# Zero matmuls in all early waits of TensorE, a replanned instruction order, and token-order stores for the last batch, in an attention + MoE kernel

## Chip, cores, metric

One core of a Trainium2 chip; each job ran on one chip, and the jobs on several. The metric is device microseconds of one execution. Each profile is one execution, and its times count from the start of the span, which is some 1.8 us shorter than the measured time. The record calls every execution but one fast; the one called slow is of the kernel before (408.87 us at a mean granted TensorE clock of 0.98, which is the share of full clock that the throttle gave, in the job of e5 to e8), and ratios use fast runs alone. But the fast state still holds executions with a mean clock of 0.97 to 0.99; where a few tenths of a per cent matter, I give the clock and compare executions of 0.996 and more.

## The reference, cut to what matters

```python
# q, k, v: (8 batches, 12 heads, 448 tokens, 64), fp32
scores = q @ k.transpose(0, 1, 3, 2) / sqrt(64)
attn = exp(scores - max); attn = attn / attn.sum(-1)
x = (attn @ v).transpose(0, 2, 1, 3).reshape(3584, 768)
h = x @ w_in                      # 768 x 2048
out = (h * sigmoid(h)) @ w_out    # 2048 x 768
```

## The kernel before

Attention is cut into **units**: four heads of one batch, all 448 tokens (two pieces of 224 in the first batch). A unit takes, in order: K and Q turned on VectorE (KT, QT); scores on TensorE into one of two score banks (s); an exponential on ScalarE, which frees the bank (E); row sums and values on TensorE (a, "a<-E,ones" and "a<-E,V"); on VectorE the sums turned, inverted and turned back (sT, inv, rdn) and two products a x rdn = xT, which also free the banks of a. Then come the MoE matmuls (h<-xT,w_in_t), tanh and gate, and the products p and o, for which VectorE also makes combinations of weights (D) and of gates (S, G, X) so that fewer matmuls are needed.

No order is written by hand. While the program is built, a planner in Python simulates the engines with fixed durations and priorities and writes down in which order each engine gets its instructions:

```python
def act(n): return n * 0.000833 + 0.093      # planned length of a ScalarE instruction
...
elif best is None or at + op.bias < best[0]: # the ready instruction with the lowest (ready time + bias) goes next
    best = (at + op.bias, op)
...
op = Op("DVE", 0.72, lambda: turn_k(b, hg), [ld_k[(b, hg)]], 20)             # bias 20: late
od.add(Op("DVE", ..., lambda n=n, c=c: add_e(n, c), deps, -1))               # T = E + E
Op("DVE", busy, lambda step=step: inverse(n, step), made[-1:] + before[step], -1)   # sT, inv, rdn
Op("DVE", ..., lambda: norm(n, part), [op] + rdn_op[n], -1, then=m_ring.give)       # xT
...
# TensorE has nothing to do, early on: zeros keep its clock up
if warm["on"] and od.free["PE"] <= od.now and wait > 0.1 and od.now > 1.0:
    n = max(1, int((wait - 0.06) / mm(128)))
    od.on_pe(Op("PE", n * mm(128), lambda n=n: run_zeros(n)), "full")
```

Results go out per 32 tokens, because tokens are kept in an interleaved order:

```python
for w in range(4):                           # one tile of 128 tokens x 384
    eng = nc.scalar if w % 2 and 4 * qd + 4 == NT * B else nc.sync
    eng.dma_start(out=dst[col // 32], in_=ost_t[(qd, i, j)][32 * w : 32 * (w + 1), :])
```

The softmax here doesn't subtract the row's maximum and nothing guards it: scores larger than these inputs give would overflow.

## Time and profile before

| | before |
|---|---|
| time, median of 3 (range) | 403.28 us (403.15 to 403.38) |
| span of the profiled execution | 401.82 us |
| first scores / V landed / first matmul that reads V | 7.44 / 15.29 / 15.38 |
| 55th MoE matmul starts | 37.63 |
| last matmul ends | 396.92 |
| last add ends / last store lands / end | 397.52 / 400.54 / 401.82 |

How to read it: TensorE is busy 98% of the span, so I cut the span at points that both kernels have in common. Up to the first matmul that reads V the loads decide; from there to the 55th MoE matmul the attention of the first units; from there to the last matmul the real work of both kernels is the same (340.75 us of streaming); then comes the tail. In the third stretch I count two things besides streaming: changes between packings of the array (from matmuls that use it whole to matmuls that use strips of 32 of its rows or columns, or back; some 0.09 us each), and waits (bursts whose start comes over 0.25 us later than the columns ahead of it explain, less one change). These are sums over the trace's matmuls, so they are larger than the waits view alone, which gives the idle time without the latencies at its ends. The lines are in the prediction below.

### The profile page before, as it was taken

Reading aid. Unit: us, or ns where it says so; the run is one execution under the profiler, and the core shown is the slowest. Engines: PE = TensorE matmul, PEld = TensorE weight load, DVE = VectorE, ACT = ScalarE, POOL = GpSimd, SP = SyncE. Lnnn points to the kernel's source line nnn. Section 1 sums busy time; section 2 is a strip of 40 time slices with the busy share of each in tenths; the row PEclk is TensorE's granted clock in tenths of the full one; section 3 lists DMA queues with packets and bytes.
Section 4 is the critical chain, followed back from the end, with each engine's and each line's share of the span. In section 5 each row is a group of like instructions: output and inputs, shape, how many; then the busy total and the mean of one; then the engine's idle time right before and its main releaser. Section 6 shows DMA issues by size and latency. Waiting matters only on the chain.

```text
span 401.8 us, 9398 instructions
## 1 busy us (share of the span) xinstructions
PE 392.6 (98%) x3758; PEld 201.9 (50%) x3758; DVE 301.1 (75%) x646; ACT 234.2 (58%) x360; POOL 88.7 (22%) x160
## 2 busy tenths in 40 slices
PE   8999999999999999999999999999999999999995
PEld 7676754444444444444445444444345555555562
DVE  2566677999997986998866985986985765775763
ACT  3887886686865769457367519738767124123410
POOL 6643466523006350300170104300000000000000
PEclk9999999999999999999999999999999999999999
DMA  7999999947017943641191537411001220122014
GB/s 115 194 199 206 164 166 206 156 71 117 2 46 120 186 57 50 112 80 47 41 150 37 105 75 93 69 41 41 2 0 42 60 59 2 40 67 53 2 39 118
DMA packets 38506, 34.42 MB, mean 86 GB/s; under 512 B 11712, under 2 KB 37696, under 8 KB 38464
## 3 DMA queue, kind: packets, MB, share of 16 engines
q0 software_dynamic: 27712, 22.82, 39.2%
q1 hardware_dynamic: 10368, 10.63, 10.5%
q8 instruction: 29, 0.48, 0.5%
q10 hardware_dynamic: 384, 0.39, 0.4%
q14 instruction: 13, 0.11, 0.1%
HBM read 45.61 MB, written 11.01 MB: 141 GB/s over the span
## 4 chain that ended last, share of the span: by engine, by line
PE 92%; DMA 2%; DVE 2%; POOL 1%; ACT 1%; issue 1%; DVEq 0%; POOLq 0%
PE h L454 37%; PE p L545 30%; PE a L383 11%; PE s L319 11%; PE o L559 3%; DMA V<-in_v_dram 2%; ACT E L356 1%; DVE T L367 1%; POOL rk L237 0%; POOL rq L243 0%; DVE G L535 0%; DVE xT L440 0%; POOL V L256 0%; DVE ost L598 0%; ACT th L465 0%
## 5 line engine op out<-in xcount | busy, mean ns | idle before, releaser
L356 ACT ACTIVATE E<-s 128x896 f16<-128x896 f32 (+1 forms) x172 | 149.2, 914 | 47.5 <-PE s L319 46.2
L454 PE MATMUL h<-xT,w_in_t 128*128 128x448 f16 (+1 forms) x864 | 156.5, 332 | 0.1
L454 PEld LDWEIGHTS <-w_in_t 128*128 128x128 f16 x864 | 79.9, 98 | 70.5 <-issue 16.4
L465 ACT ACTIVATE th<-h 128x448 f16<-128x448 f32 (+1 forms) x144 | 71.6, 505 | 68.3 <-PE h L454 62.5
L501 DVE SCALAR_TENSOR_TENSOR G<-th,h 128x448 f16<-128x448 f16 (+2 forms) x144 | 75.3, 532 | 37.4 <-ACT th L465 35.9
L256 POOL DMA_DIRECT2D V<-in_v_dram x88 | 48.7, 570 | 101.6 <-PE a L383 86.6
L319 PE MATMUL s<-QT,KT 32*128 32x448 f16 (+4 forms) x864 | 55.1, 340 | 1.2 <-ACT E L356 1.2
L545 PEld LDWEIGHTS <-G 128*128 128x128 f16 x384 | 36.4, 98 | 29.1 <-issue 5.5
L545 PEld LDWEIGHTS <-S 128*128 128x128 f16 x312 | 29.1, 98 | 23.8 <-issue 5.8
L383 PE MATMUL a<-E,V 128*32 128x448 f16 (+3 forms) x864 | 40.3, 334 | 0.7 <-DMA V<-in_v_dram 0.7
L545 PE MATMUL p<-D,G 128*128 128x384 f16 x208 | 38.0, 326 | 0.4 <-DVE xT L440 0.4
L545 PE MATMUL p<-w_out_t,S 128*128 128x384 f16 x208 | 37.0, 326 | 0.0
L440 DVE SCALAR_TENSOR_TENSOR xT<-a,rdn 128x448 f16<-128x448 f32 (+1 forms) x54 | 28.9, 561 | 9.0 <-PE a L383 8.1
L545 PE MATMUL p<-w_out_t,G 128*128 128x384 f16 x176 | 31.8, 326 | 0.0
L367 DVE TENSOR_TENSOR T<-T,E 128x1792 f16<-128x1792 f16 x20 | 21.8, 1088 | 12.8 <-ACT E L356 12.7
L319 PEld LDWEIGHTS <-KT 32*128 32x128 f16 (+2 forms) x864 | 16.6, 98 | 28.2 <-issue 27.2
L383 PEld LDWEIGHTS <-V 128*32 128x32 f16 (+2 forms) x864 | 18.3, 95 | 23.4 <-issue 14.6
L367 DVE TENSOR_TENSOR T<-E,E 128x1792 f16<-128x1792 f16 x20 | 21.7, 1084 | 6.1 <-ACT E L356 6.0
L535 DVE TENSOR_TENSOR S<-G 128x512 f16<-128x512 f16 x70 | 25.1, 415 | 0.7 <-PE p L545 0.7
L237 POOL DMA_DIRECT2D rk<-in_k_dram x24 | 13.7, 569 | 54.1 <-DVE KT L293 46.5
L293 DVE STREAM_TRANSPOSE KT<-rk 128x256 f32<-128x256 f32 (+3 forms) x48 | 16.5, 382 | 7.5 <-DMA rk<-in_k_dram 7.0
L423 DVE STREAM_TRANSPOSE sT<-a 128x448 f32<-128x448 f32 (+1 forms) x27 | 15.8, 586 | 4.8 <-PE a L383 4.4
(41 smaller groups left out, 251.9 us busy)
## 6 DMA issues: line engine op xcount, KB each, us to landing
out_dram<-ost SPq DMA_DIRECT2D x216, 48.0 KB, 1.6
rk<-in_k_dram POOLq DMA_DIRECT2D x24, 224.0 KB, 5.2
rq<-in_q_dram POOLq DMA_DIRECT2D x21, 224.0 KB, 5.8
w_out_t<-in_moe_w_out_dram POOLq DMA_DIRECT2D x8, 384.0 KB, 11.7
V<-in_v_dram POOLq DMA_DIRECT2D x43, 64.0 KB, 4.5
V<-in_v_dram POOLq DMA_DIRECT2D x40, 48.0 KB, 4.1
w_in_t<-in_moe_w_in_dram POOLq DMA_DIRECT2D x6, 256.0 KB, 7.6
w_in_t<-in_moe_w_in_dram POOLq DMA_DIRECT2D x3, 512.0 KB, 13.1
```

What stands on the lines that cost most here:

```text
L256: nc.gpsimd.dma_start(out=VT[b].rearrange("p h c i e -> p h c (i e)")[32 * x : 32 * (x + 1), hs, 0:count], in_=v[b, hs].rearrange("h (i g) ...
L293: nc.vector.transpose(out=turned.rearrange("p c x i -> p x c i")[:, x:y, 0:count], in_=t[:, first : first + count * (y - x)].rearrange("p ...
L319: nc.tensor.matmul(out=pS[p0 : p0 + 32 * (x1 - x0), h % 2, at : at + nq], lhsT=KT[(b, hg)][32 * h : 32 * (h + 1), c, x0:x1, :, e], rhs=QT[ ...
L356: nc.scalar.activation(out=E[(n, w)][0:kr, 2 * y : 2 * y + 2, 0:nk], in_=pS_t[(n, w, y)][0:kr, :, 0:nk], func=AF.Exp, scale=attn_scale,)
L367: nc.vector.tensor_tensor(out=T_t[n], in0=E[(n, 0)] if c == 1 else T_t[n], in1=E[(n, c)], op=ALU.add,)
L383: nc.tensor.matmul(out=a[32 * h : 32 * (h + 1), 0:nq], lhsT=w, rhs=e[k0:k1, h, at : at + nq], start=start, stop=stop,)
L440: nc.vector.scalar_tensor_tensor(out=xT[(b, cc)][:, 32 * g0 : 32 * g1], in0=acc[(n, part)][:, 0:nq], scalar=0.5, in1=rdn_t[n].rearrange("p ...
L454: nc.tensor.matmul(out=h[:, 0 : t1 - t0], lhsT=w_in_t[:, cc, 128 * f : 128 * (f + 1)], rhs=xT[(b, cc)][:, t0:t1], start=(cc == 0), stop=(c ...
L465: nc.scalar.activation(out=th, in_=h_t[(b, f, t0)][:, 0 : t1 - t0], func=AF.Tanh)
L501: nc.vector.scalar_tensor_tensor(out=dst[:, f, at + lo : at + hi], in0=th_t[(b, f, t0)][:, lo - t0 : hi - t0], scalar=1.0, in1=h_t[(b, f, ...
L535: nc.vector.tensor_tensor(out=dst[:, f0:f1], in0=x[:, f0:f1], in1=y[:, f0:f1], op=op)
L545: nc.tensor.matmul(out=pr_t[(qd, BANK[m])][:, 0:OH], lhsT=w[:, f, :], rhs=W_[m][:, f, :], start=(f == 0 and BANK[m] == m), stop=(f == HF - 1),
```

## The change

Its intent: no idle TensorE before the MoE runs (zeros in every gap, but only 47 ahead of the first scores), an order planned with durations nearer to the chip's and with V later, and fewer, larger stores at the end. The diff, cut to its core:

```diff
 def act(n):
-    return n * 0.000833 + 0.093
+    return n * 0.000833 + 0.065
-    PACE = 3.4
+    PACE = 3.6
 # load_q: the last batch in token order, one load for each head
+        if b == B - 1:
+            for h in range(HG): nc.gpsimd.dma_start(out=t[32*h : 32*(h+1)], in_=q[b, HG*hg+h].rearrange("(g i) d -> i g d", i=32))
 # store: contiguous tokens
+            if b == B - 1:
+                n = 2 if last and i == j else 4 - w
+                dst = out[b * S + col : b * S + col + 32 * n, cols]
+            (nc.scalar if last and w else nc.sync).dma_start(out=dst, in_=ost_t[(qd, i, j)][32 * w : 32 * (w + n), :])
 # planner: V's load 1.12 times as long in the first batch, Q's loads of the last batch four times as long;
 # the first K turned in two parts, the first burst of scores undivided
 # biases on VectorE:
-turns of K and Q 20   combine_w 30   combine_g 0   add_e -1   inverse -1   norm (xT) -1    gate -0.3
+turns of K and Q  8   combine_w 100  combine_g 8   add_e  0   inverse  4   norm (xT) -10   gate -2
 # biases on ScalarE:
-tanh -2    copies -2
+tanh -0.3  copies -0.3
-                od.now >= pace["next"] or moe_i is None or len(moe) < 30
+                od.now >= pace["next"] or moe_i is None or len(moe) < 14
-                pace["next"] = min(max(pace["next"], od.now - 4), od.now) + ...
+                pace["next"] = min(max(pace["next"], od.now - 8), od.now) + ...
+                    if av_seq[0][0][0] < 9 and (x := qk_at()) is not None and x <= od.now + 0:
+                        break                       # scores ahead of values, first units
+    FIRST_ZEROS = 47
+    od.on_pe(Op("PE", FIRST_ZEROS * 2 * mm(128), lambda: run_zeros(FIRST_ZEROS)), "full")
-        if ... wait > 0.1 ...:      n = max(1, int((wait - 0.06) / mm(128)))
+        if ... wait > 0.05 ...:     n = max(1, int((wait - -0.06) / each))    # each: twice as long before 8 us
```

(The two lines of biases sum up single numbers that stand at their instructions.)

## The prediction

> **What bounds the kernel now.** I read the page first (busy shares, chain by engine), then the timeline of the first 30 us, the chain of waits up to 40 us, the waits of TensorE alone from 37.7 us on, and the timeline and the stores of the last 6 us.
>
> ```profile
> PE 392.6 (98%) x3758; PEld 201.9 (50%) x3758; DVE 301.1 (75%) x646; ACT 234.2 (58%) x360; POOL 88.7 (22%) x160
> ...
> PE 92%; DMA 2%; DVE 2%; POOL 1%; ACT 1%; issue 1%; DVEq 0%; POOLq 0%
> ```
>
> TensorE is the bound, and it is nearly gapless. So the change can only win where TensorE does no useful work: before V lands, at a few waits, at changes between packings of the array, and behind the last matmul. No matmul with data in it is removed.
>
> ```profile
> 1.03 6.47 PE L1157 MATMUL z<-zeros 128*128 128x128 f16 x73 [1.03 <-DVE zeros L214]
> ...
> 5.09 0.70 DVE L293 STREAM_TRANSPOSE KT<-rk 128x384 f32<-128x384 f32 x2 [4.12 <-DMA rk<-in_k_dram]
> 5.72 0.37 DVE L304 STREAM_TRANSPOSE QT<-rq 128x224 f32<-128x224 f32 x1
> ...
> 7.44 0.60 PE L319 MATMUL s<-QT,KT 32*128 32x224 f16 x16
> ...
> 8.05 7.62 ACT L356 ACTIVATE E<-s 128x896 f16<-128x896 f32 x9 [6.03 <-PE s L319]
> ...
> 15.38 0.57 PE L383 MATMUL a<-E,V 128*32 128x224 f16 x16 [0.69 <-DMA V<-in_v_dram]
> ...
> 16.49 0.92 ACT L356 ACTIVATE E<-s 128x896 f16<-128x896 f32 x1 [0.82 <-PE s L319]
> ```
>
> Two things stand in it. The first scores could start at about 6.1, when K and Q have been turned (5.72 + 0.37), but wait until 7.44 behind 73 zero matmuls. And whatever is won there meets a wall: V is not there before 15.0.
>
> ```profile
> 5.77 9.24 DMA V<-in_v_dram
> ...
> 34.18 0.81 ACT E L356
> ...
> 35.03 0.38 PE a L383 x6
> ...
> 37.53 0.83 PE h L454 x7
> ```
>
> The chain up to 40 us runs through the landing of V, not through the zeros or the first exponentials. From V on it is TensorE, then a second knot at 33 to 37.5: two exponentials of the sixth unit, its row sums, the chain of VectorE to its xT, and the MoE matmuls that need it.
>
> ```profile
> PE s L319 <- ACT E L356: 0.8, 2, 0.5
> PE p L545 <- DVE xT L440: 0.4, 1, 0.4
> ```
>
> These are all waits of TensorE after 37.7 that the waits view gives; with the latency at their ends they cost about 0.9 (at 57.8), 0.65 (at 77.7) and 0.55 (at 123.0), 2.1 us in all.
>
> ```profile
> 395.68 3.65 SPq L593 DMA_DIRECT2D out_dram<-ost  x7
> ...
> 396.73 1.74 ACTq L593 DMA_DIRECT2D out_dram<-ost  x4
> ...
> 396.96 0.56 DVE L598 TENSOR_TENSOR ost<-p,s 128x384 f32<-128x384 f32 x1 [0.26 <-PE p L545]
> ...
> DMA to landing us min/median/max: 1.5/1.7/2.0
> ```
> The last result is in SBUF at 397.52, yet the sync queue issues stores until 399.33; the last starts at 398.9, lands some 1.6 later at 400.5, and 1.3 us of closing follow.
>
> **What the Trainium skill says.** "TensorE: Matmul & The Clock Gate", section "What's actually happening": the array starts at half clock and gets the full one after about one window of 3.4 us of activity, and the window runs free of the kernel's start. The trace agrees in kind: the 73 zeros take 6.41 us, not 73 x 0.056 = 4.1, so about 44 of them ran at 0.107 (44 x 0.107 + 29 x 0.056 = 6.3); here it took 4.7 us. "Back-to-back issue gap" on that page gives columns / 2.4 GHz + 2.5 ns for a warm matmul; the trace agrees (448 columns every 0.189 us). "DMA: Bandwidth & Descriptors", section "Issuing engines are not separate DMA queues": several issuing engines save only issue time; section "Why small descriptors are slow (HBM only)": 256-byte pieces pay a fixed overhead each. The first fits the end of this trace, where issue time is what is queued; no load here has 256-byte source rows, so the second is not shown yet.
>
> **Part by part, start.** 47 zeros in place of 73: 44 cold and 3 warm are 44 x 0.107 + 3 x 0.056 = 4.9 us from 1.03, so they end near 5.95, still before Q is turned; K turned in two parts lets Q through some 0.3 earlier. The first scores then start near 6.1, **1.3 us earlier**. The loads, though, are issued in the same order with the same waits, so V should land at 15.0 again, and the built order has exactly the same real matmuls ahead of the first one that reads V (nine score bursts and one row sum). All of the 1.3 us turns into waiting, whether filled with zeros (93 of the 96 now stand before that point or in front of it) or not. After V I walked the new order burst by burst with the lengths of the old timeline (two score halves 0.70, 16 value matmuls 0.44, 32 of them 0.88, a half score burst 0.50 to 0.53, an exponential every 0.814): the first MoE matmul comes near 22.05 in place of 22.70, since one alternation of scores and values is gone and scores run in pairs. But the new order does all eight first MoE tiles before the sixth unit's row sums, so the two exponentials there lie bare: scores to 32.9, exponentials to 34.75, sums at 34.8 against 35.03. From there on the work left is again identical in both kernels (340.75 us of streaming). So of 1.3 us about **0.25** arrives.
>
> **Middle.** From there to the last matmul the old kernel takes 359.3 us: 340.75 streaming, 2.1 of waits, and 16.4 that 186 changes of packing account for, 0.088 each (a check: 24 MoE matmuls of 224 columns should take 2.30 and the next scores start 2.40 after them). The built order now has 189 changes: **+0.27**. For waits I looked for scores that follow scores too closely. A burst needs both score banks back, which is two exponentials: about 2.4 us from start to start (75.99 to 78.38). The old order has pairs planned 1.70 and 1.72 apart, and those are its two score waits. The new one has the same two, and two more of 1.87 and 2.0. That makes about 2.25 us of waits: 0.7 + 0.65 + 0.5 + 0.4. The xT wait at 123 (0.55) should go, as xT now comes first on VectorE. Middle together about **+0.4**. Against that, the planner's figures are nearer to the chip: an exponential of 896 is planned at 0.811 (it was 0.839; measured 0.814), so orders chosen with it should hold fewer waits that I don't see. For this I take off **0.4**, as a judgement.
>
> **Last batch.** Q in token order takes four loads in place of one for three units, in 256-byte pieces: 9 more issues of about 0.57 on GpSimd. The old kernel loads the last Q at 254.8 and turns it at 282.8; 28 us of slack hide that. K and V need no order. The stores get contiguous tokens: the last four tiles go as 8 stores less. The last two tiles take one store of 96 KB on each of two queues, issued at once when the last add ends. That puts the last landing at about 2.2 us after the add (1.7 to 2.0 for 48 KB, plus some 0.3 for twice the bytes), where it was 3.0: **-0.8**.
>
> **Sum.** 403.28 - 0.25 + 0.4 - 0.4 - 0.8 = 402.2.
>
> **Rivals.** (1) The early start carries through: -1.3 in place of -0.25, total about 401.1. For it: in both kernels TensorE is full from V on. Against: same work before V, same V. It needs V to land earlier, and nothing issued before V changes. (2) The new order removes nearly all waits, as it was made with better figures: another -1.8, near 400.5. For it: two of the figures were clearly off (cold zeros, exponentials). Against: the same close pairs are in the new order, and tanh (0.455 to 0.50 for 448 columns, planned 0.438) and the copies (0.505, planned 0.385) are now planned further from the truth. (3) A wait replaces a wait: the bare exponentials before the sixth unit and the two new close pairs cost more than I give them, or lower priority for sums on VectorE starves products: +1 to +1.5, so 403.5. (4) The tail gains little since a store of 96 KB takes as long as two of 48: +0.5.
>
> **Range and chances.** The sizes are all below 2 us and partly cancel; I give each of start, middle and tail an error of 0.5 to 0.9, so 400.7 to 403.6. Two per cent is 8.1 us. Even without a wait after V: 15.4, then 355.7 of streaming, some 213 changes at 0.088, 2.3 for the half-packed score bursts of the first units, 4.1 from the last matmul to the end and 1.5 that the measured time has over the span (403.28 against 401.8) make 397.7. So faster by over 2% (under 395.2) is next to impossible, and nothing in sight costs 8 us either.
>
> **What would show it.** Right: first scores near 6.1, V again at 15.0 to 15.4, first MoE matmul near 22, the sixth unit's sums ending near 35.1, score waits near 46, 58 and 78, last landing 2.0 to 2.4 after the last add. Wrong: a V that lands at another time, the sixth unit's knot passed over 0.7 us earlier or later, TensorE waits after 37.7 of under 1 or over 3.5 us in sum, or a last store still queued behind others.

## The result, and the profile after

**404.77 us** median of 4 (404.38 to 405.50), where the kernel before took 403.21 (402.74 to 403.38) beside it: 1.0043 times as long, 95% interval 1.0024 to 1.0061. Ratios here are the mean time of one kernel's fast runs over that of the other's of the same rounds, so not quite the ratio of the medians quoted. By the measure of 2% that is "same"; against the prediction it is 2.6 us late and 1.2 us outside the range.

| us | before | after | difference | predicted |
|---|---|---|---|---|
| first scores | 7.44 | 5.72 | -1.72 | -1.3 |
| first matmul that reads V | 15.38 | 14.47 | -0.91 | 0 |
| from there to the 55th MoE matmul | 22.25 | 22.97 | **+0.72** | -0.25 |
| from there to the end of the last matmul | 359.30 | 361.06 | **+1.76** | 0.0 (+0.4 - 0.4) |
| last matmul to the end of the span | 4.90 | 4.17 | -0.73 | -0.8 |
| span | 401.82 | 402.67 | +0.85 | -1.05 |

The rows from "reads V" on sum to the last: -0.91 + 0.72 + 1.76 - 0.73 = +0.84. The -0.91 is not the change's doing: in the profiles of kernels that load in this order (15 of the 17 here), V's last part lands anywhere from 14.0 to 15.6.

Timeline of TensorE in the kernel after (start, length, engine, line, operation, tiles, shapes, count, and in brackets the idle time ahead and what ended it):

```profile
1.03 4.22 PE L1186 MATMUL z<-zeros 128*128 128x128 f16 x47 [1.03 <-DVE zeros L214]
5.72 0.58 PE L330 MATMUL s<-QT,KT 32*128 32x224 f16 x16 [0.47 <-DVE QT L315]
...
14.47 0.57 PE L394 MATMUL a<-E,V 128*32 128x224 f16 x16 [0.57 <-DMA V<-in_v_dram]
...
19.73 0.76 PE L394 MATMUL a<-E,V 128*32 128x224 f16 x22
21.14 0.47 PE L394 MATMUL a<-E,V 128*32 128x224 f16 x10 [0.65 <-issue]
21.54 0.60 PE L330 MATMUL s<-QT,KT 32*96 32x224 f16 x8
22.07 1.32 PE L465 MATMUL h<-xT,w_in_t 128*128 128x224 f16 x12
...
34.83 0.37 PE L394 MATMUL a<-E,ones 96*32 96x224 f16 x6 [0.53 <-ACT E L367]
```

The scores start when Q is there, and V is the wall again: TensorE stands 0.57 before it even with zeros. New is the line with `[0.65 <-issue]`: in the middle of a burst of 32 equal matmuls TensorE stands for 0.65 us, and nothing that the profile shows holds it. The kernel before runs the same kind of burst in one piece.

Waits of TensorE from 37.5 us on, kernel after (who waits, for whom, us in total, times, longest); the same view of before had two lines, 0.8 and 0.4:

```profile
PE h L465 <- DVE xT L451: 1.3, 3, 1.0
PE a L394 <- DVE xT L451: 0.5, 1, 0.5
PE p L556 <- DVE S L546: 0.3, 1, 0.3
PE h L465 <- DVE sT L434: 0.3, 1, 0.3
PE s L330 <- ACT E L367: 0.2, 1, 0.2
```

ScalarE was the first cause before; now all but 0.2 is VectorE. With the latencies at their ends the waits come to 3.58 us in place of 2.12, and there are 189 changes of packing in place of 186: 1.46 + 3 x 0.09 = 1.73 of the 1.76. The largest is at 76.7. VectorE there, kernel after:

```profile
74.99 0.64 DVE L304 STREAM_TRANSPOSE KT<-rk 128x256 f32<-128x256 f32 x2
76.37 0.62 DVE L451 SCALAR_TENSOR_TENSOR xT<-a,rdn 128x448 f16<-128x448 f32 x1 [0.74 <-PE a L394]
76.91 0.64 DVE L443 STREAM_TRANSPOSE rdn<-inv 128x448 f32<-128x448 f32 x1
77.47 0.60 DVE L315 STREAM_TRANSPOSE QT<-rq 128x448 f32<-128x448 f32 x1
78.00 1.12 DVE L451 SCALAR_TENSOR_TENSOR xT<-a,rdn 128x448 f16<-128x448 f32 x2
```

TensorE meanwhile, kernel after:

```profile
76.75 0.93 PE L465 MATMUL h<-xT,w_in_t 128*128 128x448 f16 x4
78.64 0.35 PE L465 MATMUL h<-xT,w_in_t 128*128 128x448 f16 x1 [0.96 <-DVE xT L451]
79.17 0.35 PE L465 MATMUL h<-xT,w_in_t 128*128 128x448 f16 x1 [0.18 <-DVE xT L451]
```

VectorE idles 0.74 before the first xT, though the turn of the reciprocals (rdn) that the next two xT need could have run there. It does that turn, and the turn of a Q that nobody needs yet, between them instead. The kernel before had the turn ahead, and its three xT in one piece:

```profile
74.59 0.64 DVE L432 STREAM_TRANSPOSE rdn<-inv 128x448 f32<-128x448 f32 x1
75.16 0.66 DVE L293 STREAM_TRANSPOSE KT<-rk 128x256 f32<-128x256 f32 x2
75.74 1.65 DVE L440 SCALAR_TENSOR_TENSOR xT<-a,rdn 128x448 f16<-128x448 f32 x3
```

The tail, kernel after. First the last add, then the issues of the last 8 us (count, KB each, median us to landing):

```profile
398.53 0.56 DVE L615 TENSOR_TENSOR ost<-p,s 128x384 f32<-128x384 f32 x1 [0.27 <-PE p L556]
```

```profile
out_dram<-ost SPq DMA_DIRECT2D x3, 96.0 KB, 2.1
...
out_dram<-ost ACTq DMA_DIRECT2D x2, 96.0 KB, 2.4
```

The add ends at 399.09; the last store lands 2.48 after it (3.02 before), and the closing takes 1.10 (1.28 before).

### The profile page after: what moved, and what is told of

It reads as the page before. It is cut to its first block, busy times and chain, and to the rows that moved or that the text cites. A ratio compares the mean times of both kernels' runs of the same rounds, so it can differ in the third digit from the quotient of the medians.

```text
span 402.7 us, 9371 instructions
## 1 busy us (share of the span) xinstructions
PE 391.7 (97%) x3752; PEld 200.2 (50%) x3752; DVE 301.4 (75%) x647; ACT 234.3 (58%) x360; POOL 94.5 (23%) x169
## 3 DMA queue, kind: packets, MB, share of 16 engines
HBM read 45.61 MB, written 11.01 MB: 141 GB/s over the span
## 4 chain that ended last, share of the span: by engine, by line
PE 89%; DVE 3%; DMA 2%; issue 1%; ACT 1%; POOL 1%; ACTq 0%; DVEq 0%; POOLq 0%
PE h L465 36%; PE p L556 29%; PE a L394 12%; PE s L330 10%; PE o L570 3%; DMA V<-in_v_dram 2%; ACT E L367 1%; DVE xT L451 1%; DVE QT L315 1%; POOL rk L237 0%; POOL rq L251 0%; DVE S L546 0%; DVE KT L304 0%; POOL V L264 0%; DVE sT L434 0%
## 5 line engine op out<-in xcount | busy, mean ns | idle before, releaser
L330 PE MATMUL s<-QT,KT 32*128 32x448 f16 (+4 forms) x864 | 54.2, 340 | 0.9 <-DVE QT L315 0.5
L546 DVE TENSOR_TENSOR S<-G 128x512 f16<-128x512 f16 x70 | 26.3, 415 | 0.7 <-PE p L556 0.6
L237 POOL DMA_DIRECT2D rk<-in_k_dram x24 | 13.7, 572 | 42.0 <-DVE KT L304 36.5
L625 ACT COPY ost<-p 128x384 f32<-128x384 f32 x13 | 6.3, 481 | 29.6 <-DMA out_dram<-ost 15.4
L304 DVE STREAM_TRANSPOSE KT<-rk 128x192 f32<-128x192 f32 (+3 forms) x49 | 16.7, 378 | 5.9 <-DMA rk<-in_k_dram 5.9
```

What stands on the lines that cost most here:

```text
L304: nc.vector.transpose(out=turned.rearrange("p c x i -> p x c i")[:, x:y, c0 : min(c1, count)], in_=t[:, first : first + count * (y - x)].r ...
L330: nc.tensor.matmul(out=pS[p0 : p0 + 32 * (x1 - x0), h % 2, at : at + nq], lhsT=KT[(b, hg)][32 * h : 32 * (h + 1), c, x0:x1, :, e], rhs=QT[ ...
L546: nc.vector.tensor_tensor(out=dst[:, f0:f1], in0=x[:, f0:f1], in1=y[:, f0:f1], op=op)
```

## The experiments

Fifteen kernels ran, all with correct results. The stretches of their profiles, in us (a clock of one half for 17 us is in the row of e6):

| kernel | reads V at | to 55th MoE matmul | to last matmul | waits in it | to the end |
|---|---|---|---|---|---|
| before | 15.38 | 22.25 | 359.30 | 2.12 | 4.90 |
| after | 14.47 | 22.97 | 361.06 | 3.58 | 4.17 |
| e11 after again | 14.88 | 23.62 | 361.06 | 3.58 | 4.15 |
| e1 tail only | 14.60 | 22.24 | 359.27 | 2.11 | 4.15 |
| e4 / e12 start and tail, old plan | 14.51 / 15.12 | 22.45 / 22.27 | 359.27 / 359.28 | 2.13 / 2.13 | 4.19 / 4.21 |
| e2 old VectorE biases | 15.02 | 23.35 | 361.72 | 4.89 | 4.19 |
| e3 old ScalarE biases and pace | 14.46 | 22.62 | 361.50 | 3.53 | 4.15 |
| e5 three moved | 14.78 | 23.32 | 360.39 | 2.98 | 4.15 |
| e9 one moved ahead | 14.69 | 22.67 | 360.55 | 3.05 | 4.16 |
| e10 one moved back | 14.71 | 22.26 | 359.73 | 2.55 | 4.24 |
| e6 no filling zeros | 15.64 | 26.78 | 359.27 | 2.12 | 4.15 |
| e7 more zeros, old start | 15.92 | 22.87 | 359.27 | 2.12 | 4.94 |
| e8 V loaded first | 13.02 | 26.58 | 359.63 | 2.36 | 4.14 |
| e15 the same, weights earlier | 12.64 | 24.94 | 359.39 | 2.11 | 4.15 |
| e13 20 zeros fewer | 14.11 | 22.93 | 361.06 | 3.58 | 4.15 |
| e14 12 zeros more | 15.69 | 22.76 | 361.06 | 3.58 | 4.14 |

The third stretch repeats to 0.01 to 0.03 us between profiles of one order, on different chips. So differences of 0.3 there are of the order, though an execution's time scatters by 1 us.

### The tail alone (e1)

```diff
 # the kernel before, with load_q() and store() of the kernel after; nothing else
```

> The kernel before with only the last batch's part: its Q in token order by four loads, its tokens stored in order in larger stores. The built order of matmuls and of VectorE is the same as before, instruction by instruction. Theory (the tail wins on its own): the changed kernel's profile has the last landing 2.48 us after the last add where it was 3.02, so about 0.5 us faster than before, 402.7, with the same waits of TensorE. Rival (the 256-byte loads of Q or the larger stores cost what the shorter queue wins): 403.2 or more.

The kernel took 402.72 us median (402.02 to 405.81, 6 runs); before on that chip 404.02 (402.95 to 408.94, 11 runs), ratio 0.9964 (0.9911 to 1.0017), with dips of the clock in both. The four executions at 0.997 and more took 402.02 to 402.90, those of before 402.95 to 404.02. In the profile the end comes 4.15 after the last matmul in place of 4.90. **The tail is worth 0.75**, as predicted. V came 0.78 earlier in this profile, with the same order on every engine, and the 55th MoE matmul 0.79 earlier: what lies between follows V one to one.

### Start and tail with the old plan (e4, e12), beside the kernel after (e11)

```diff
 # the kernel after, with the old numbers again:
-act 0.065, PACE 3.6, limits -8 and 14, V x 1.12, the break for scores, the nine VectorE and three ScalarE biases
+act 0.093, PACE 3.4, limits -4 and 30, V x 1,    none,                 the old biases
 # kept: 47 zeros first, zeros in every wait, the first K in two parts, the tail
```

> Both sets of planning constants set back at once: what stays of the change is the zeros (47 first, thresholds), K turned in two parts with the first score burst undivided, and the last batch's part. Theory: the early start is swallowed by the landing of V (0 to 0.3 us arrive), the tail gives 0.5: about 402.5, with the waits at 58, 78 and 123 as in the kernel before. Rival (the early start carries through, 1.3 us): 401.4.

> The old plan with the new start and tail once more, on the same chip as the kernel after. Theory: 402.3 within 0.3, no execution with a mean clock under 0.996, 359.27 between the 55th MoE matmul and the last, and faster than the kernel before on the same chip by 0.8 to 1.2 us in the executions of full clock. Rival: it comes within 0.3 of the kernel before.

> The kernel after itself, beside the old plan on one chip. Theory (the new plan costs 1.8 us and keeps start and tail): 1.5 to 2.3 us over e12 of this job in medians, 361.0 to 361.3 between the 55th MoE matmul and the last, and no execution with a mean clock below 0.996, as the zeros keep the clock. Rival (the difference is of the chip or of chance): under 0.8 us over e12.

e4: 402.32 us (402.01 to 402.76), ratio 0.9937 (0.9891 to 0.9982) to a kernel before that dipped in 5 of 11 executions. e12 and e11, side by side on another chip: **402.83** (402.65 to 403.48) and **404.55** (404.14 to 405.48), with before at 403.49 (402.64 to 408.43). The 1.72 between these medians is what the replanning costs. In the profiles the third stretch alone differs by 1.78 (361.06 - 359.28); it is 361.06 on both chips that the kernel after was profiled on, so the loss is no accident of a run. The old plan with the new start and tail beats both kernels: the medians of e4 and e12 lie 1.1 and 0.6 below the medians of before's executions at full clock on the same chips (403.46 and 403.45). e12 missed the 402.3 expected, by 0.2 more than the margin, and its gain over before at full clock was 0.6, under the 0.8 expected.

### Which half of the new numbers (e2, e3)

```diff
 # e2: the kernel after, VectorE's biases alone as before
-turns 8   combine_w 100  combine_g 8  add_e 0   inverse 4   norm -10  gate -2
+turns 20  combine_w 30   combine_g 0  add_e -1  inverse -1  norm -1   gate -0.3
 # e3: the kernel after, all else of the plan as before
-act 0.065, PACE 3.6, limits -8 and 14, ScalarE biases -0.3, V x 1.12, break
+act 0.093, PACE 3.4, limits -4 and 30, ScalarE biases -2
```

> The changed kernel with the nine priorities of VectorE's work set back to the old ones (turns 20, weight sums 30, sums of G 0, sum of E -1, inverse -1, xT -1, gate -0.3); all else as changed. Theory (the new VectorE priorities put turns and sums of E ahead of the inverse and xT, and TensorE waits for these: 1.6 us at 76.75, 0.6 at 53.9, 0.6 at 118.1, 0.35 at 149.7): those waits go, the waits of TensorE after 37.5 us fall from 3.75 to about 2 us, and the time to about 403.0. Rival (the waits come from the other planning constants or are spread by chance over any new order): 404.3 or more, with new waits of the same total elsewhere.

> The changed kernel with the other planning constants set back (ScalarE's length 0.093, pace 3.4 with its limits 4 and 30, ScalarE's priorities -2, V's 1.12 and the break in the value loop out), the new VectorE priorities kept. Theory (VectorE's priorities are the cause): stays near 404.5, with waits on xT, sT or S of 1.5 us or more in TensorE after 38 us. Rival (pace and ScalarE constants are the cause): near 403.0.

e2 405.35 us (404.90 to 406.04), ratio 1.0011 (0.9965 to 1.0057); e3 404.35 (403.94 to 405.09), ratio 0.9987 (0.9937 to 1.0038). **Neither half alone gives the time back**: 361.72 and 361.50 in the third stretch, and the 403.0 that e2's theory expected did not come. They differ in which waits they hold. e3 keeps the 1.47 (at 75.9) and the 0.49 for S, so VectorE's new biases make those. e2 has them down to 0.41 and none, but gets 1.34 at 205.9 and 0.65 at 239.7, which no other order has. And e2 still has the wait of 0.5 of the values for xT near 54 (0.61 with its latency), which e3 and e12 have not: that one comes with the other new numbers, in which TensorE splits that burst of values around scores. Each set of numbers was tuned with the other. (No single number was set back in a run; which of the nine VectorE biases does it stays open.)

### Moving instructions, not numbers (e5, e9, e10)

To have the suspected cause alone, I changed the finished list and left all other orders as they were.

```diff
 # e5: kernel after                            # e9: kernel after            # e10: kernel e4
+move(rdn of unit 8, before xT of unit 7, 2nd) +move(rdn of unit 8, before..) +move(rdn of unit 8, AFTER xT of unit 7, 2nd)
+move(QT of unit 11, after xT of unit 8, 2nd)
+move(S of gates, before KT of unit 15)
```

> The changed kernel with three VectorE instructions moved and nothing else: the second reciprocal spread (rdn) ahead of the xT before it, the turn of Q at 77.5 behind the two xT, and one sum of G ahead of the turn of K at 117. Orders on all other engines are the same, instruction by instruction. Theory (VectorE's order is what TensorE waits for at 76.75 and 118.1): the wait of 1.47 falls to about 0.4 and that of 0.48 to 0, so the stretch from the 55th MoE matmul to the last one falls from 361.06 to about 359.6, and the time by 1.3 to 1.5 us to about 403.3. Rival (these waits only take the place of others further on, on ScalarE or banks): the stretch stays above 360.6.

> The kernel after with one instruction moved and nothing else: VectorE's turn of the reciprocals of unit 8 (0.64 us) goes ahead of the product xT_3 in place of behind it, at 76 us. Theory (the 1.47 us wait is VectorE's order): the turn then runs at about 75.6, while VectorE has nothing to do (it waits 0.74 for sums of TensorE there), so the two products behind it come 0.55 earlier: the wait of the MoE matmuls at 77 goes from 1.47 to about 0.95, and the time from the 55th MoE matmul to the last matmul from 361.06 to 360.5. Rival (waits only move on, as in the run where three instructions were moved and half of the gain came back): the wait shrinks, but the sum stays within 0.15 of 361.06.

> The mirror image, on the kernel with the old plan, the new start and the new tail: the same turn of the reciprocals goes behind the product xT_3. Theory: the products behind it come 0.55 later, the wait of the MoE matmuls at 76 goes from 0.42 (and 0.26 at the next scores) to about 0.95 to 1.0, and the time from the 55th MoE matmul to the last matmul from 359.27 to 359.6 to 359.9. Rival: later slack takes it in, the sum stays within 0.15 of 359.27.

**e9**, VectorE and TensorE:

```profile
75.48 0.60 DVE L445 STREAM_TRANSPOSE rdn<-inv 128x448 f32<-128x448 f32 x1
76.30 0.62 DVE L453 SCALAR_TENSOR_TENSOR xT<-a,rdn 128x448 f16<-128x448 f32 x1 [0.21 <-PE a L396]
```

```profile
78.04 0.35 PE L467 MATMUL h<-xT,w_in_t 128*128 128x448 f16 x1 [0.44 <-DVE xT L453]
```

The turn now fills VectorE's idle time, of which 0.21 is left, and TensorE's idle time falls from 0.96 to 0.44 (with latencies from 1.47 to 0.95). The stretch fell by **0.51**, to 360.55, and all other waits stayed: the theory's number. **e10**, the mirror image on the good plan, VectorE:

```profile
75.46 0.62 DVE L453 SCALAR_TENSOR_TENSOR xT<-a,rdn 128x448 f16<-128x448 f32 x1 [0.74 <-PE a L396]
76.00 0.63 DVE L445 STREAM_TRANSPOSE rdn<-inv 128x448 f32<-128x448 f32 x1
```

VectorE idles the same 0.74 as in the kernel after, and the stretch grew by **0.45**, to 359.73. One instruction of 0.64 us behind its neighbour in place of ahead costs TensorE half a microsecond; it is shown both ways. In time neither is visible beyond the scatter (e9 404.19, 403.77 to 406.32, against e11's 404.55; e10 402.79, 402.35 to 403.99, against e12's 402.83).

e5 moves two more instructions. It took 404.25 us (403.72 to 405.87). The wait at 77 fell from 1.47 to 0.41, and the 0.48 for S went. But 0.50 came up at 119.5 and 0.18 at 89.6, and 0.26 at the scores behind the first place. So 0.67 of the 1.54 taken away was left; more than half came back further on. Both the theory and its rival were partly right there.

### What the zeros are for (e6, e7)

```diff
 # e6: kernel e4, no zeros after the first 47
-            od.on_pe(Op("PE", n * each, lambda n=n: run_zeros(n)), "full")
+            od.on_pe(Op("PE", n * each, lambda: None), "full")
 # e7: the kernel before, 20 zeros more: 16 in place of 8 after the first scores, 12 ahead of the first values
```

> The kernel with the changed start and tail on the old planning constants (402.3), without the zero matmuls after the first 47; all other orders the same. Theory (the zeros between the first scores serve the clock only: in the last runs the kernels with the old start had 7 of 17 executions with a mean granted clock under 0.996 and 2 to 5 us longer, those with the new start none of 22): many executions show a clock of 0.98 to 0.995 and 404 to 409 us, and if the profile is one of them, a stretch at half clock in the first 25 us. Rival (the clock drops come from the chip and not from idle TensorE): 402.3 with a clock of 0.998 to 1.

> The kernel before with 20 zero matmuls more: 16 in place of 8 after the first scores, and 12 ahead of the first values, in the two gaps of 0.45 and 0.7 us that TensorE had there; late start, order and tail as before. Theory (filling is what holds the clock): no execution under a clock of 0.996, and 403.0 to 403.6 throughout, where the kernel before on the same chip has some at 405 to 409. Rival (the clock is held by the start at another time, or drops by chance of the chip): as many slow executions as the kernel before has in the same rounds.

e6: 405.16 us (403.04 to 407.61, ratio 1.0015, 0.9959 to 1.0072), and all six executions ran at a mean clock of 0.972 to 0.990. Its profile by stretches (length, busy time and instructions of each engine, then granted clock, DMA share, GB/s):

```profile
4.00:11.00 7.00, 4.65 (x85) 3.40 (x84) 3.29 (x11) 4.14 (x5) 4.17 (x8) 1.00 1.14 161
11.00:28.00 17.00, 14.24 (x215) 9.33 (x211) 6.46 (x19) 8.38 (x11) 11.13 (x17) 0.50 1.24 201
```

The clock was full from 4.18, fell to half at 11.01 and stayed there for 17.1 us; the 55th MoE matmul came at 42.42, 5.5 later than in e4. TensorE was busy for 66% of the stretch ahead of the drop (94% in the kernel before), and its longest pause there was 1.00 us. **So the filling is needed**: without it the median is 2.8 us longer (405.16 against the 402.32 of e4, on another chip), though its fastest execution (403.04, clock 0.990) is as fast as the kernel before. The clock dips at times in the kernel before too: of its 51 executions over all jobs 11 had a mean clock of 0.98 to 0.993 and took 405.95 to 408.94 us. Of the 56 executions of kernels with the new start, all its zeros and the loads in the old order (after, e2 to e5, e9 to e12, e14) none was under 0.996; three stood at 0.996 (405.16 and 405.87 in e5, 406.32 in e9) and may hold a short dip. The zeros are no guarantee: e8 below has all of them too, 66 after the first 47, and two of its six executions ran at 0.990 and 0.994 (408.10 and 405.57 us). In its profile TensorE stood 1.22 before V. So far as these runs go, steadiness is what the new start with its filling buys besides, and I had not thought of it.

e7 shows why the zeros need the early start: no execution under 0.996 (0.996 to 0.999), as its theory had it, but the 403.0 to 403.6 expected did not come: V's matmuls start at 15.92 though V had landed at 14.51, and it took 404.26 us (403.44 to 405.04) against 403.57 (ratio 0.9999, 0.9955 to 1.0042). Old start and full filling don't fit ahead of V. (Six executions are few: with dips in 11 of 51, six without one are no proof for the added zeros.)

### Is V alone the wall? (e8, e15)

```diff
 # kernel e4: V's loads ahead of the third K and Q
-    for hg in range(NG):   plan_k(0, hg); plan_q(hg)
+    for hg in range(NG - 1): plan_k(0, hg); plan_q(hg)
     plan_v(0, 0, NG)
+    plan_k(0, NG - 1); plan_q(NG - 1)
```

> The kernel with the changed start and tail on the old planning constants, with V loaded ahead of the third K and Q. Theory (V's landing is the wall of the start): the first value matmul comes about 3 us earlier, near 11.5, and at least half of that reaches the 55th MoE matmul: 36.96 falls below 35.9, the time to 401.3 or less. Rival (the start is bound by the loads as a whole, or by ScalarE's exponentials, and V is only the first to show it): the 55th MoE matmul stays within 0.5 us of 36.9, and the time near 402.3.

e8: V landed at 12.88, 1.5 earlier than in e4 (first used at 13.02, not near 11.5), and the 55th MoE matmul came at 39.60, **2.6 later**; 405.91 us (405.15 to 408.10), ratio 1.0048 (1.0002 to 1.0094). But the trace shows that it did not put the question cleanly. GpSimd in e8, which issues all loads in one order:

```profile
9.79 0.53 POOL L251 DMA_DIRECT2D rq<-in_q_dram  x1 [0.60 <-DVE QT L315]
15.61 0.53 POOL L251 DMA_DIRECT2D rq<-in_q_dram  x1 [5.29 <-DVE QT L315]
16.13 4.19 POOL L277 DMA_DIRECT2D w_in_t<-in_moe_w_in_dram  x6
```

A Q load stood 5.29 us before a buffer that only the turn of the third Q frees, which now lands later (14.36), and the weights behind it stood with it: their third part landed at 24.75 in place of 21.16, and the first MoE matmuls waited 0.90 for it. So e15 takes this away:

```diff
 # e8, with the weights ahead of those Q loads
-    for n in range(NG, min(2 * NG, NB0)): plan_q(n)
-    plan_w_in(0, DFF // 4)
+    plan_q(NG)
+    plan_w_in(0, DFF // 4)
+    for n in range(NG + 1, NB0): plan_q(n)
```

> As e8 (V loaded ahead of the third K and Q), but the first weights w_in go ahead of the Q loads of the first batch that wait for a free buffer. In e8 GpSimd stood 5.3 us at such a load while the queues ran empty, the weights landed 3.6 later than in e4, and the first MoE matmuls waited 0.90 for them; so e8 does not tell whether V alone is the wall. Theory (the wall is all early loads, the third K comes next): V lands near 12.9 again, the weights no longer hold anything, but the 55th MoE matmul comes at 38 to 39, still 1 to 2 us after that of e4 (36.96), as scores of the third group cannot start before its K, landing near 14. Rival (V alone is the wall, and e8 lost only by the blocked issue): the 55th MoE matmul comes at 35.5 to 36.5, and the time is near 401.5.

V landed at 12.50, no weight was waited for, and the 55th MoE matmul came at 37.58, where e4 and e12 have 36.96 and 37.39: **V 1.9 and 2.5 us earlier brought nothing.** In e15 the third K lands at 13.70 in place of 9.89 in e4. It took 402.73 us (402.56 to 405.87, ratio 0.9984, 0.9905 to 1.0062), no better than e4 and e12. The rival's 35.5 to 36.5 is out; the theory's 38 to 39 was 0.4 too late. V is a wall as the last of the early loads; with V moved ahead, the third K came last. (That this K alone sets the 37.58 was not tested.)

### The wait that the profile does not explain (e13, e14)

In every profile with a wait inside a burst near 21 us, it lay behind the same matmul of the program (350th from its start; the expectations call it the 349th, counting from zero), whatever that matmul was. The profile lists a DMA queue with 29 reads of 16 KB (`q8 instruction: 29, 0.48, 0.5%`); whose instructions they bring it does not say. The Trainium skill, "Runtime: NRT & Kernel Launch", section "Instruction fetch mechanics", says that an engine's instructions are read in blocks of 16 KiB (256 instructions) while it runs, and that crossing into a new block is "mostly hidden". So I moved the position, not the work:

```diff
 # the kernel after; zeros of each filling, in the order of the plan
+    FILL = [2, 1, 1, 4, 2, 2, 2, 2, 2, 4, 2, 2, 3, 0, 0, 0, 0, 0, 0, 0]    # e13: 20 fewer
+    FILL = [2, 1, 1, 4, 2, 2, 2, 2, 2, 4, 2, 2, 5, 2, 4, 2, 2, 2, 15, 3]   # e14: 12 more
-            od.on_pe(Op("PE", n * each, lambda n=n: run_zeros(n)), "full")
+            od.on_pe(Op("PE", n * each, lambda n=n: run_zeros(FILL.pop(0))), "full")
```

> The kernel after without 20 of its 49 filling zeros (the second half of the third filling before V, all later ones); every other instruction and order is the same. Theory (instructions not there yet): in every profile with a stall of TensorE inside a burst near 21, it begins behind the 349th matmul of the program, zeros counted, and ends 1.3 to 1.5 us after the second read on the instruction queue (landing near 19.6 to 20.9). With 20 zeros less the 349th matmul is 20 real ones further on, some 1 us of work later: no stall is left, or at most 0.3 where the read lands late; from the first matmul with V to the 55th MoE matmul it takes 22.3 to 22.5 us where the kernel after took 22.97 and 23.62. Rival (the stall belongs to that burst of values: its exponentials or a bank): it stands behind the same value matmul, the 22nd of its burst, as before, and the stretch takes 22.9 to 23.6. Side expectation: mean clock still 0.996 or more, as the long fillings ahead stay; if not, the zeros that I took were needed.

> The kernel after with 12 zeros more in the last filling before V, every other order the same. Theory (instructions not there yet): the stall begins behind the 349th matmul of the program again, which is now the 10th value matmul of the burst in place of the 22nd, and ends 1.3 to 1.5 us after the second read on the instruction queue; the stretch from the first matmul with V to the 55th MoE matmul is 22.9 to 24. Rival: the stall stays behind the 22nd value matmul of the burst, or goes.

TensorE in e13:

```profile
21.27 0.37 PE L465 MATMUL h<-xT,w_in_t 128*128 128x224 f16 x2
21.89 1.12 PE L465 MATMUL h<-xT,w_in_t 128*128 128x224 f16 x10 [0.26 <-issue]
```

TensorE in e14:

```profile
20.95 0.47 PE L394 MATMUL a<-E,V 128*32 128x224 f16 x10
21.85 0.76 PE L394 MATMUL a<-E,V 96*32 96x224 f16 x22 [0.43 <-issue]
```

With 20 zeros fewer the wait moved out of the values and into the first MoE burst, and with 12 more it moved from behind the 22nd value matmul to behind the 10th: **it follows the count of instructions, not the work.** That TensorE waits there for the read is inferred from this and from the time: the wait ended 1.28 and 1.50 us after the second read of the instruction queue had landed (20.62 and 20.35). In the kernel after, its repeat, e2, e3, e5 and e9 that was 1.29 to 1.54. What remains without the wait is nearly the same: after 22.97 - 0.65, e11 23.62 - 1.30, e9 22.67 - 0.34, e14 22.76 - 0.43 all give 22.32 to 22.33 (e13 22.67), where the kernel before has 22.25 and no wait. Orders made with the old numbers stand at the edge too: behind the same matmul TensorE idled 0.24 in e3 and 0.09 in e4. When the read landed, at 19.6 in both, the kernel before had 301 matmuls behind it and after 328. The zeros are not more there (96 in the kernel after, 102 before). But V was earlier that time, and the new order gets to the 350th matmul 5.8 us after the first one that reads V (after, e11, e9, e2, e5), where before takes 6.2 and the old plan with the new start 6.4. So the lead that hid the reading is gone. Why the reading did not come sooner was not tested. That the DMA engines are full then fits: in e8, where they moved only 32 GB/s from 14 to 16 us (200 in the kernel after), it landed at 17.59, with 265 matmuls started.

Two expectations missed. The stretch of e13 was 22.93, not 22.3 to 22.5; its V came at 14.02, the earliest of all, and the exponentials behind it did not, which I have not followed further. And one of its four executions fell to a clock of 0.989 (407.07 us), so the zeros that I took out were needed. e13 took 405.20 us (404.03 to 407.07), e14 405.59 (404.42 to 405.88), before 403.10; the stretch of e14 was 0.14 under what I had given.

## Why the prediction was wrong, by its own steps

1. **The start reaches V, and V is a wall: right.** First scores came at 5.7 to 6.3 (6.8 in e14), and nothing of that 1.3 us passed V. e1 shows the one-to-one dependence on V, e15 that V stands for the early loads as a whole.
2. **"Only 0.25 of 1.3 us arrives": wrong.** The order after V did as walked in its own terms (the sixth unit's sums ended at 35.2, predicted 35.1), but only because V landed 0.9 early that time. That was luck: the loads were as before. Counted from V, the new order costs 0.07 plus the wait inside a burst near 21, of 0.34 to 1.30 (22.67 to 23.62 in place of 22.25). I counted the real matmuls ahead of each point and found them equal, walked bursts and exponentials, and did not ask whether the instructions themselves would be there, which by e13 and e14 they seem not to have been. This term was off by 0.7 to 1.6 us.
3. **Changes of packing, +0.27: right** (186 to 189).
4. **"The xT wait at 123 should go, as xT now comes first on VectorE": the step that failed most.** The wait at 123 did go. But I read the bias of -10 as if an xT could be ready early. What it needs, rdn, had gone from -1 to +4, and the turns of K and Q from 20 to 8, nearer to it. So first place went to an instruction that stood behind two others, rdn and a QT: 1.47 at 76.7. And TensorE waited 0.48 at 118.1 for S, which stood behind two turns: its bias had gone from 0 to 8, where theirs now is too. The waits came to 3.58 where I had about 2.25. e3 and e2 show that VectorE's biases make the 1.47 and the 0.48; e9 and e10 show one instruction of it both ways. The 0.61 at 53.9, also for an xT, is not of these biases, as e2 has it and e3 has not; it was not tested by itself. Of the four score waits that I named from pairs too close together, only the one at 58 came.
5. **"-0.4, as the planner's figures are nearer to the chip": wrong in sign.** The replanning as a whole costs 1.72 (e11 against e12). In this planner better figures for some durations gave no better order; the figures were not tested apart from the biases and limits.
6. **The tail, -0.8: right in sum (-0.73, and -0.75 in e1), in part by luck.** The stores gave only 0.54: the last one landed 2.48 after the add, not 2.2, and past the 2.0 to 2.4 that I had set, as a store of 96 KB took up to 2.45 from issue to landing. The other 0.18 is the closing, 1.10 in place of 1.28, which I had left alone; it is 1.28 in e7 and 1.1 in e1 and e4, so it goes with the new tail, for a reason not looked into. What the 256-byte pieces cost in Q's loads no run separates; no wait for them shows.

In the sum: -0.25 + 0.0 - 0.8 = -1.05 was predicted; apart from where V lands it was +0.72 + 1.76 - 0.73 = +1.75 in the first profile. My third rival had the right kind, "a wait replaces a wait", and named VectorE's sums; I put it at 1 to 1.5 and did not think of a loss at the start on top of it. The sign of "wrong" that I set, over 3.5 us of waits after 37.7, was reached.

## What to carry to other kernels

Here a high priority for xT was worth no more than the priorities of its inputs: when you raise the last link of a chain, walk the whole chain back in the built order and see where the engine idles ahead of it. When you pack an early stretch more densely while loads keep the DMA queues full, ask whether the supply of instructions is the next limit: a wait for nothing visible that stays at one count of instructions is the sign, and zeros added or taken out move it. And split a change by undoing its parts: here the good parts (tail, zeros) with the old order beat both kernels, at 402.3 and 402.8 us, while the whole was slower.

## What the Trainium skill lacked or had wrong

- "Runtime: NRT & Kernel Launch", "Instruction fetch mechanics", calls the crossing into a new block mostly hidden and explains it by dispatch being slower than filling. Here TensorE waited 0.09 to 1.30 us at one place in its instructions (e13 and e14 show that it keeps to their count), with the DMA engines moving some 200 GB/s, and went on 1.3 to 1.5 us after the 16 KB read had landed. That many short matmuls with a busy DMA might outrun the reading, as is inferred here, is not said there.
- "TensorE: Matmul & The Clock Gate", "What's actually happening", gives an idle window of some 3.4 us as what brings the clock down (a later section of the page tells of frequent short pauses that make it swing, without their share). In e6 it fell with no pause over 1.00 us, after a stretch that was 66% busy, while e14, 76% busy over the same 4 to 11 us and with a pause of 1.45, kept it; in e6 it then stayed at half for 17.1 us although TensorE was busy 84% of them. The times between its changes, 6.83 and 17.07, do fit two and five of the page's windows of 3.413 us. How busy a window must be the page does not give.
- No page says how many zeros keep a clock: with 49 to 61 in the waits up to 20 us none of 56 executions fell under a mean of 0.996, but with 66 two of 6 did (e8; in e15, with 66 too, none of 4); with 29 one of 4 (e13) and 13 of 57 (before and e1), with none all 6 (e6).
